# Scores by pairs of heads on two column groups, a fixed order for the first loads, and one piece per kept part of w_in, in an attention + MLP kernel

## The chip, the cores and the metric

The kernel runs on one core of a Trainium2 chip. A core has five engines that run side by side, each with its own queue of instructions in a fixed order: TensorE (PE, matmuls), VectorE (DVE), ScalarE (ACT), GpSimd (POOL) and SyncE (SP, here the main issuer of DMAs). They synchronise through semaphores. DMAs are issued from the queue of an engine and carried out by 16 shared DMA engines. The metric is the device time of one execution in microseconds, lower is better.

## The reference

Inputs are q, k, v of shape 8 x 8 x 576 x 64 (batch, heads, tokens, head size), phi of 8 x 8 x 576 x 32, w_in of 512 x 2048 and w_out of 2048 x 512, all float32.

```python
a    = softmax(phi, axis=memory)                  # 32 memory slots per head
k_m  = einsum('bhsm,bhsd->bhmd', a, k);  v_m = einsum('bhsm,bhsd->bhmd', a, v)
attn = softmax(q @ k_m.T / sqrt(64))              # 576 x 32 per head
x    = (attn @ v_m), heads side by side           # 4608 tokens x 512
out  = relu(x @ w_in) ** 2 @ w_out                # 4608 x 512
```

(The weights arrive as float64 bit patterns, each number as two 32-bit words; the kernel makes from each number a float32 high part and a low part.)

## The kernel before

**Algebra.** The value side is folded into the weights: instead of attn @ v_m and then @ w_in, the kernel makes `vw = v_m @ w_in` per batch (lines 500 to 546) and multiplies the attention probabilities with it. Large products are made of three float32r matmuls (high x high, low x high, high x low), so most tiles exist as a high and a low part (`ah`/`al`, `gh`/`glo`, `V[:, 0]`/`V[:, 1]`).

**Work units.** A *memory unit* `memory(b, hh)` (line 392) treats four heads of batch b: it loads phi, k and v, takes a softmax over phi, and forms k_m and v_m for the four heads with tiled matmuls: in `pk`, heads s = 0 to 3 write to rows 32s to 32s + 31, on four column groups (`tile_position=(0, 32 * s)`, line 426). The sums over tokens are made at L439, L442 or, for odd batches, L445, where two 64-column groups are used. For batches 0 and 1 (lines 455 to 472) k_m and v_m of the four heads are spread into `kvx` with zeros (times `halves`), turned by two transposes into `pv`, and the first block becomes `kbd`, a 128 x 128 matrix with the key memory of two heads on the diagonal. For batches 2 to 7 (473 to 484) k_m goes through `kvn` and a DVE transpose into `kT`; only v_m is turned by PE. `values` copies the turned v_m into `VT` parts. All memory units and the scores of batches 1 to 7 share one PSUM bank, `pa`, in the order in which the program makes them.

**Scores.** For batches 0 and 1 `first_attention` (588) loads q by head in 256-byte rows (L602) and the last 64 tokens apart (L595), turns q with PE (L613), multiplies with `kbd` (L636, L648), takes the softmax (line 678) and turns the result back (L664, L671) to `ath` and `atl`. For batches 2 to 7 `scores` (551) loads q of four heads in two DMAs with one row of 18 tokens x 64 numbers per partition (L557), turns it with DVE in 32 x 32 blocks (`qT`, L569), makes `kb` from `kT` and a mask (L562), and runs, for each half of the tokens (8 and 10 blocks of 32, so 256 and 320 columns), two matmuls of all 128 rows and columns that add up in PSUM (`psc`, L574): one per half of the head size. DVE turns the scores to token rows (L578), softmax follows, and DVE turns back (L703).

**MLP.** `step(g)` does `mm1` (L740: `h` = attention x vw, then relu and square on ACT and DVE) and `mm2` (L770, L771, L773: adds to four accumulators) for one batch and one of 16 blocks of 128 hidden columns. `mm2_left` (L796) treats the left-over 64 tokens of two batches together.

**Weights.** `decode(kind, j, h, room)` (307) loads a 512 KB piece of raw weights (L322) and makes the two parts with five DVE steps, ACT and, for the first pieces, PE (L350 to L352). The parts of w_out stay in SBUF. Those of w_in are stored to two DRAM tensors, `w_in_hi` and `w_in_lo`, by two DMAs on POOL's queue per piece (L364), and `wi_again` (366) loads them again with two DMAs per piece (L369), in rows of 1 KB, for batch 1 and each later pair of batches.

**Order.** Nothing runs in the order of the code. `Plan` (53) collects every operation with its cost per engine, then `order()` (111) simulates the engines: each takes the ready operation with the smallest `late` time (propagated back from its users, or set by `cap`), less `LEAD` for operations marked `lead`. The resulting order is what is issued. A DMA is an operation of the engine that issues it; it costs 620 ns of that engine's queue (1250 if `two`), passes a wire of 240 bytes per ns and lands `LANDS` later. At the start all loads without a predecessor are ready at once, so `late` alone orders them: phi, k, v of the first memory unit, phi of the second, two raw pieces of w_in, k and v of the second unit, q of batch 0, raw w_out, the left-over q.

## Time and profile before

| | us |
|---|---|
| median of three timed runs (lowest, highest) | 816.61 (813.18, 818.7) |
| the profiled execution's own time | 816.34 |
| its span, first to last instruction | 814.6 |
| PE busy | 776.2 |
| DVE busy | 536.4 |
| ACT busy | 403.1 |
| mean granted PE clock | 0.994 |

How to read the profile: PE is matmuls, PEld its weight loads, SPq DMA issue on SP's queue. `L574` is line 574 of the kernel. A row of a group gives out<-in by tile names, shapes, the count, then busy time in us and the mean length of one in ns, then idle time of the engine just before. A row of the timeline gives start and length in us; `x4` means that four instructions were merged, and a bracket gives the idle time before and what ended it. A matmul of plain float32 is two MATMUL instructions. Lengths of matmuls include pipelining and overlap, so the cost of one is read from start to start.

### The profile page before, as it was taken

What the parts mean: (1) busy time and instruction counts of PE and PEld (TensorE: products, weight loads), DVE (VectorE), ACT (ScalarE), POOL (GpSimd) and SP (SyncE); (2) the same over time, 40 slices, a digit from 0 to 9 for tenths busy, and PEclk for the clock granted to TensorE, in tenths of its full rate; (3) what the DMA queues carried; (4) which work ended last, traced back from release to release, by engine and by line L of the source; (5) the groups of instructions that cost most, each with busy time, mean ns of one, the idle gap of its engine ahead of it and who ended that gap; (6) DMA issues with size and microseconds to landing.
All of it is one profiled execution on the core that took longest, in us unless ns stands there. A gap on an engine that the chain in (4) does not pass through costs nothing.

```text
span 814.6 us, 13267 instructions
## 1 busy us (share of the span) xinstructions
PE 776.2 (95%) x4926; PEld 652.5 (80%) x4926; DVE 536.4 (66%) x1190; ACT 403.1 (49%) x922; POOL 63.8 (8%) x103
## 2 busy tenths in 40 slices
PE   4889999999999999999999999999999999999995
PEld 2567888778887888888778888888788888888884
DVE  4678888783468976766776556877677556864540
ACT  2557766675653465634445355644334355643220
POOL 4012202320100100010000100010000100000000
PEclk9999999999999999999999999999999999999998
DMA  7969967666456523423443433513422433100001
GB/s 225 270 191 286 270 176 239 188 170 191 125 146 189 165 81 105 129 37 90 132 125 88 126 106 104 136 34 91 133 58 70 122 108 104 30 24 29 1 1 64
DMA packets 99716, 101.04 MB, mean 124 GB/s; under 512 B 32260, under 2 KB 85508, under 8 KB 99652
## 3 DMA queue, kind: packets, MB, share of 16 engines
q1 hardware_dynamic: 89188, 81.55, 34.2%
q0 software_dynamic: 10464, 18.65, 8.8%
q8 instruction: 39, 0.64, 0.3%
q14 instruction: 25, 0.20, 0.1%
HBM read 79.17 MB, written 17.83 MB: 119 GB/s over the span
## 4 chain that ended last, share of the span: by engine, by line
PE 73%; DVE 8%; issue 6%; DMA 5%; ACT 4%; SPq 1%; POOL 1%; DVEq 0%; POOLq 0%; ACTq 0%
PE h L740 20%; PE acc L770 12%; PE acc L773 12%; PE acc L771 12%; PE accl L796 5%; PE pvw L536 4%; PE psc L574 3%; PE pkv L426 2%; DMA raw<-in_moe_w_out_dram 1%; DMA phi<-in_phi_dram 1%; ACT vw L260 1%; DMA raw<-in_moe_w_in_dram 1%; DMA wo<-work 1%; DVE glo L750 1%; DVE work L327 1%
## 5 line engine op out<-in xcount | busy, mean ns | idle before, releaser
L740 PE MATMUL h<-ath,vw 128*128 128x320 f32 (+1 forms) x1024 | 211.6, 298 | 1.1 <-ACT r L744 0.6
L770 PE MATMUL acc<-wo,gh 128*128 128x512 f32 x512 | 207.0, 404 | 1.8 <-ACT gh L746 1.6
L771 PE MATMUL acc<-wo,gh 128*128 128x512 f32 x512 | 201.7, 394 | 0.0
L740 PEld LDWEIGHTS h<-ath,vw 128*128 128x128 f32 x1024 | 171.0, 189 | 17.2 <-ACT r L744 1.7
L773 PE MATMUL acc<-wo,glo 128*128 128x512 f32 x512 | 162.1, 405 | 1.7 <-DVE glo L750 1.5
L260 ACT CAST vw<-pvw 64x256 fp32r<-64x256 f32 (+1 forms) x224 | 85.7, 397 | 74.5 <-PE pvw L536 35.4
L545 DVE TENSOR_TENSOR vw<-pvw,vw 64x256 fp32r<-64x256 f32 x192 | 78.8, 420 | 64.8 <-ACT vw L260 62.9
L770 PEld LDWEIGHTS acc<-wo,gh 128*128 128x128 f32 x512 | 96.4, 188 | 23.4 <-ACT gh L746 3.7
L740 PE MATMUL h<-atl,vw 128*128 128x320 f32 (+1 forms) x512 | 109.9, 295 | 0.0
L771 PEld LDWEIGHTS acc<-wo,gh 128*128 128x128 f32 x512 | 96.4, 188 | 16.6
L773 PEld LDWEIGHTS acc<-wo,glo 128*128 128x128 f32 x512 | 89.5, 189 | 19.5 <-DVE glo L750 6.2
L746 ACT ACTIVATE gh<-r 128x512 fp32r<-128x512 f32 x128 | 80.8, 632 | 43.4 <-DVE r L745 37.6
L750 DVE TENSOR_TENSOR glo<-r,gh 128x512 fp32r<-128x512 f32 x128 | 87.5, 684 | 21.4 <-ACT r L748 19.7
L744 ACT ACTIVATE r<-h 128x256 f32<-128x256 f32 (+1 forms) x149 | 60.1, 406 | 56.8 <-PE h L740 53.5
L745 DVE TENSOR_SCALAR r<-h 128x320 f32<-128x320 f32 (+1 forms) x107 | 48.9, 459 | 58.4 <-PE h L740 57.9
L740 PEld LDWEIGHTS h<-atl,vw 128*128 128x128 f32 x512 | 82.5, 189 | 0.7 <-issue 0.2
L747 ACT ACTIVATE gl<-r 128x64 fp32r<-128x64 f32 x128 | 32.8, 256 | 68.5 <-DVE r L745 66.5
L748 ACT ACTIVATE r<-r 128x576 f32<-128x576 f32 x94 | 64.5, 686 | 2.2
L796 PE MATMUL accl<-wo,gl 128*128 128x512 f32 x192 | 52.3, 397 | 0.1
L796 PEld LDWEIGHTS accl<-wo,gl 128*128 128x128 f32 x192 | 35.0, 188 | 7.2 <-DVE o L260 0.5
L536 PE MATMUL pvw<-wi,VTh 128*128 128x256 f32 x192 | 37.3, 286 | 0.6 <-issue 0.3
L749 DVE TENSOR_TENSOR r<-r 128x576 f32<-128x576 f32 x34 | 25.7, 756 | 15.8 <-ACT gh L746 14.4
(137 smaller groups left out, 854.3 us busy)
## 6 DMA issues: line engine op xcount, KB each, us to landing
wi<-w_in_hi SPq DMA_DIRECT2D x56, 256.0 KB
wi<-w_in_lo SPq DMA_DIRECT2D x56, 256.0 KB
KV<-in_k_dram SPq DMA_DIRECT2D x32, 256.0 KB
KV<-in_v_dram SPq DMA_DIRECT2D x32, 256.0 KB
raw<-in_moe_w_in_dram SPq DMA_DIRECT2D x16, 512.0 KB
raw<-in_moe_w_out_dram SPq DMA_DIRECT2D x16, 512.0 KB
q<-in_q_dram SPq DMA_DIRECT2D x24, 288.0 KB
out_dram<-o POOLq DMA_DIRECT2D x20, 256.0 KB, 7.7
```

Source lines behind the costliest of these rows:

```text
L260: nc.scalar.copy(o, i) if e == "ACT" else ENG[e].tensor_copy(o, i)
L536: nc.tensor.matmul(pw()[:, x * SL:(x + 1) * SL], l()[:, 2 * hh + x, :], w(r, x), start=(i == 0), stop=(i == 2))
L545: vec({"DVE": tt(SL)}, lambda e, V=V, pr=pr, src=src: nc.vector.tensor_sub(V()[pr, 1, hh, :], src(), V()[pr, 0, hh, :].bitcast(F32)), [pw, ...
L740: nc.tensor.matmul(p()[:, 0:n], V()[:, l, hh, c0:c0 + P], x()[:, hh, cs], start=(i == 0), stop=(i == 5))
L744: op({"ACT": act(n) - 30, **({} if b < 2 else {"DVE": tt(n)})}, lambda e, cs=cs, n=n, p=p: nc.scalar.activation(r()[:, cs], p()[:, 0:n], A ...
L746: op({"ACT": act(SM)}, lambda e: nc.scalar.activation(gh(), r()[:, 0:SM], AF.Square), [r], [gh])
L748: op({"ACT": act(S), **({} if b < 2 else {"DVE": tt(S)})}, lambda e: nc.scalar.activation(r(), r(), AF.Square) if e == "ACT" else nc.vecto ...
L750: vec({"DVE": tt(SM)}, lambda e: nc.vector.tensor_sub(glo(), r()[:, 0:SM], gh().bitcast(F32)), [r, gh], [glo])
L770: nc.tensor.matmul(a(), gh()[:, c], t()[:, 0], start=f0, stop=False)
L771: nc.tensor.matmul(a(), gh()[:, c], t()[:, 1], start=False, stop=False)
L773: nc.tensor.matmul(a(), glo()[:, c], t()[:, 0], start=False, stop=f1)
L796: nc.tensor.matmul(a(), G()[:, l, :], t()[:, w], start=(ff == 0 and n == 0), stop=(ff == NFF - 1 and n == 2))
```

## The change

1. **Scores of batches 2 to 7** use `kbd`, as batches 0 and 1 do: the special way with `kvn`, `kT`, `vx` and `kb` goes, every memory unit makes `kvx` and two transposes, and `kbd` is kept in a buffer per batch parity and head group. q comes in another layout, `[P, 2, NC, 32]`: for each pair y and head i of the pair, two DMAs (one per half of the head size, 32 numbers) of pieces of 128 bytes, eight DMAs per unit instead of two. The two matmuls of a half no longer add up: each makes the scores of one pair of heads from all 128 rows and 64 columns of `kbd`, on its own column group (`tile_position=(0, 64 * y)`), into its own 64 rows of PSUM.
2. **First loads**: eleven names in `FIRST` give the loads a fixed order through `cap`; the two in `BESIDE` (v of the first unit, phi of the second: four and two DMAs) are issued from ACT's queue.
3. **Kept parts of w_in**: one DRAM tensor in the layout of the tile; one store per piece, when both parts are there, and one reload, in rows of 4 KB.
4. `kvx` has a buffer of its own, and some PE costs in the plan are smaller (600 to 460, 1800 to 1400, 450 to 350).

```diff
-LANDS = {"SP": 1400, "POOL": 4000}
+LANDS = {"SP": 1400, "ACT": 1400, "POOL": 4000}
...
-    def dma(fn, size, r=(), w=(), eng="SP", two=False, **more):
-        e = {"SP": nc.sync, "POOL": nc.gpsimd}[eng]
+    def dma(fn, size, r=(), w=(), eng="SP", two=False, first=None, **more):
+        q_ = {"SP": nc.sync, "ACT": nc.scalar, "POOL": nc.gpsimd}
         issue = 700 if eng == "POOL" else 1250 if two else 620
-        return op({eng: issue}, lambda _: fn(e.dma_start), r=r, w=w, size=size, lat=0, **more)
+        if first in FIRST:
+            eng = "ACT" if first in BESIDE else eng
+            more["cap"] = 10000 * FIRST.index(first) - 1e6
+        return op({eng: issue}, lambda _: fn(q_[eng].dma_start), r=r, w=w, size=size, lat=0, **more)
...
+    FIRST = ["phi 0 0", "k 0 0", "v 0 0", "phi 0 1", "k 0 1", "v 0 1", "q 0 0", "q 0 1", "ql 0", "wi 0", "wo 0"]
+    BESIDE = ["v 0 0", "phi 0 1"]
...
-            for x in (0, 1):
-                dma(lambda d, x=x: d(wi_rows(x, j, h), t()[:, x].bitcast(F32)), 2048 * P, r=[(t, (h, x))], w=[(w_in_parts[x], (j, h))], eng="POOL", lead=True)
+            dma(lambda d: d(w_in_parts()[j, h], t().rearrange("p x c f -> p (x c f)").bitcast(F32)), 4096 * P, r=[t], w=[(w_in_parts, (j, h))], eng="POOL", lead=True)
...
-        for x in (0, 1):
-            dma(lambda d, x=x: d(t()[:, x].bitcast(F32), wi_rows(x, s, hh)), 2048 * P, r=[(w_in_parts[x], (s, hh))], w=[(t, (hh, x))], lead=True)
+        dma(lambda d: d(t().rearrange("p x c f -> p (x c f)").bitcast(F32), w_in_parts()[s, hh]), 4096 * P, r=[(w_in_parts, (s, hh))], w=[t], lead=True)
...
+        op({"PE": 350}, turn_kv, [kvx], [pv], lead=True, lat=300)
+        kbd = kTs[b, hh] = st([P, P], F32, f"kb{b % 2}{hh}", f"kbd{u}")
+        op({"ACT": act(P), "DVE": tt(P)}, lambda e: copy(e, kbd(), pv()[:, 0:P]), [pv], [kbd], lead=True)
...
+    def halves_of(d, dst, src):
+        for u in (0, 1):
+            d(dst[32 * u:32 * u + 32], src[:, 32 * u:32 * u + 32].rearrange("(p c) d -> p c d", c=NC))
...
-        Q = st([P, NC * D], F32, "q", f"q{u}")
-        for x in (0, 1):
-            h0 = 4 * hh + 2 * ((x + b) % 2)
-            dma(lambda d, x=x, h0=h0: d(Q()[64 * x:64 * x + 64], q[b, h0:h0 + 2].rearrange("h (p c) d -> (h p) (c d)", c=NC)),
-                2 * S * D * 4, [], [(Q, x)], lead=True)
+        Q = st([P, 2, NC, 32], F32, "q", f"q{u}")
+        for y in (0, 1):
+            for i in (0, 1):
+                hd = 4 * hh + (2 * (y + b) + i) % 4
+                dma(lambda d, y=y, i=i, hd=hd: halves_of(d, Q()[64 * i:64 * i + 64, y], q[b, hd]), S * D * 4, [], [(Q, (y, i))], two=True, lead=True)
...
-                for x in (0, 1):
-                    nc.tensor.matmul(pq()[:, 0:32 * n], kb()[:, x].rearrange("p h m -> p (h m)"),
-                                     qT()[:, x, 0:n].rearrange("p c t -> p (c t)"), start=(x == 0), stop=(x == 1))
+                for y in (0, 1):
+                    ys = slice(64 * y, 64 * y + 64)
+                    nc.tensor.matmul(pq()[ys, 0:32 * n], kbd()[:, ys], qT()[:, y, 0:n].rearrange("p c t -> p (c t)"),
+                                     start=True, stop=True, tile_position=(0, 64 * y))
```

72 lines of the change are left out of this document (22 added, 50 removed).

## The prediction

> **What bounds the kernel now.** I read the page's busy times first, then busy time by stretch for the first 165 us, then the timeline of the start, and last the timeline around two groups of matmuls.
>
> ```profile
> PE 776.2 (95%) x4926; PEld 652.5 (80%) x4926; DVE 536.4 (66%) x1190; ACT 403.1 (49%) x922; POOL 63.8 (8%) x103
> PE   4889999999999999999999999999999999999995
> PE 73%; DVE 8%; issue 6%; DMA 5%; ACT 4%; SPq 1%; POOL 1%; DVEq 0%; POOLq 0%; ACTq 0%
> ```
>
> TensorE (PE) is the bound: 776 of 814.6 us. In the strip of 40 slices only the first three and the last are below 9. So time comes off in two ways: fewer PE microseconds anywhere after the start, or less PE idle time at the start. Relief on another engine is worth only what it gives PE. The sums below are made against the profiled execution's own 816.34 us, which is 1.7 us over its span of 814.6 and 0.27 us under the median of the three timed runs (816.61).
>
> ```profile
> core 0: us, PE busy (x) PEld busy (x) DVE busy (x) ACT busy (x) POOL busy (x), PEclk, DMA share, GB/s
> 0.00:6.00 6.00, 0.00 (x0) 0.00 (x0) 1.26 (x3) 1.59 (x2) 5.13 (x14) 1.00 0.51 140
> 6.00:15.00 9.00, 4.19 (x82) 2.67 (x82) 3.67 (x8) 1.37 (x2) 2.39 (x3) 1.00 0.85 250
> 15.00:30.00 15.00, 12.93 (x132) 8.47 (x132) 7.10 (x21) 6.42 (x13) 3.38 (x5) 1.00 1.02 292
> 30.00:49.00 19.00, 13.82 (x67) 9.16 (x68) 17.28 (x38) 11.28 (x23) 1.15 (x2) 0.91 0.97 253
> 60.00:100.00 40.00, 39.56 (x300) 31.48 (x299) 34.38 (x75) 29.75 (x64) 9.84 (x14) 1.00 0.91 274
> 100.00:165.00 65.00, 59.52 (x353) 51.59 (x351) 52.33 (x110) 44.37 (x96) 13.60 (x18) 1.00 0.70 208
> ```
>
> Each row gives the length of a stretch, busy time per engine, PE's granted clock, the busy share of the DMA engines and what they moved. Up to 49 us PE is busy 4.19 + 12.93 + 13.82 = 30.9 us, so 18 us are idle. The limit changes inside that stretch. Up to 6 us the DMA engines are half idle. From 15 to 30 us they are full while VectorE (DVE) works 7.1 of 15 us. From 30 to 49 us DVE is the limit with 17.28 of 19. Later, from 100 to 165 us, PE loses 5.5 us more while weights are decoded.
>
> ```profile
> 8.39 0.74 ACT L417 ACTIVATE phi<-phi 128x640 f32<-128x640 f32 x1 [5.98 <-DVE phi L415]
> 8.57 4.86 DMA raw<-in_moe_w_in_dram
> 11.08 1.27 DVE L409 TENSOR_REDUCE mx<-phi 128x128 f32<-128x640 f32 x1 [2.73 <-DMA phi<-in_phi_dram]
> 16.75 5.04 SPq L602 DMA_DIRECT2D q<-in_q_dram  x8
> 19.43 0.30 PE L411 MATMUL pmx<-ident,mx 128*128 128x128 f32 x1 [0.58 <-DVE VTl L494]
> 26.80 2.00 PE L636 MATMUL psc<-kbd,qT 128*128 128x64 f32 x16
> 35.46 0.82 DVE L682 TENSOR_REDUCE red<-S 128x20 f32<-128x640 f32 x1 [1.14 <-ACT S L652]
> 48.62 0.51 PE L740 MATMUL h<-ath,vw 128*128 128x256 f32 x2 [0.61 <-ACT r L744]
> ```
>
> The second line is a piece of the chain of waits, the others are the timeline (start, length). Raw weights arrive at 13.4 us, but what they feed cannot run before the attention of batch 0: its q is issued only at 16.75, its second memory unit has its maximum at 11.1 but the matmul that turns it only at 19.4 (one PSUM bank serves all memory units in turn, and the first unit's tail stood behind decode steps on DVE). Scores come at 26.8, the last softmax begins at 35.5, and `h` runs in a stream from 48.6.
>
> **The change, part by part.**
>
> *Start.* The fixed order puts phi, k, v of both memory units and q ahead of the first raw weights. Bytes from the shapes: phi 295 KB, k 590 KB and v 590 KB per unit, eight q loads of 131 KB, 131 KB of left-over q: 4.1 MB; then 1.05 MB each for `wi 0` and `wo 0`. At the 292 GB/s of the full stretch, from 2 us on, q is in by about 16 us, `wi 0` by 20 instead of 13.4, `wo 0` by 23.5. The six DMAs on ScalarE's queue cost it six issues of 5.04/8 = 0.63 us, 3.8 us in all. They lie in its idle 5.98 us ahead of the exponential at 8.39; without that cover the exponential would slip by up to 3.8 us. On SP's queue the same 3.8 us go, at a time when the DMA engines are 0.51 to 0.85 busy, so k and v of the second unit are issued earlier; what they pass are the raw weights. With no decode step on DVE before 20 us, the first unit's tail closes at about 15, the turn at 19.43 moves there, and scores and softmax come 8 to 10 us earlier; PE's queue, in order, no longer holds that turn behind the decode's matmuls. What is late next is DVE. It has idled 49 - (1.26 + 3.67 + 7.10 + 17.28) = 19.7 us by 49 us. After the change the idle part is, as an estimate, 4.7 us before phi lands plus about 6.5 us in the gaps of two memory units one after the other. The same 29.3 us of DVE work is then done about 9 us earlier, and `h` starts near 40. I take -9 us. Ends: -12 if softmax waits for nothing but q, +6.6 if the raw weights, which land 13.4 to 20 us, decide the first `h`.
>
> *Scores of batches 2 to 7.* Twelve units (six batches, two head groups), each with a half of 256 and one of 320 columns.
>
> ```profile
> 249.56 1.03 PE L574 MATMUL psc<-qT,kb 128*128 128x256 f32 x4
> 250.65 0.39 PE L771 MATMUL acc<-wo,gh 128*128 128x512 f32 x1
> 252.25 1.24 PE L574 MATMUL psc<-qT,kb 128*128 128x320 f32 x4
> 253.56 0.39 PE L771 MATMUL acc<-wo,gh 128*128 128x512 f32 x1
> 253.78 0.39 PE L770 MATMUL acc<-wo,gh 128*128 128x512 f32 x1
> 243.53 0.39 PE L773 MATMUL acc<-wo,glo 128*128 128x512 f32 x1
> 243.85 0.28 PE L445 MATMUL pkv<-ones,asum 128*64 128x1 f32 x4
> 244.41 0.40 PE L740 MATMUL h<-atl,vw 128*128 128x256 f32 x2
> 244.64 0.40 PE L740 MATMUL h<-ath,vw 128*128 128x256 f32 x2
> 244.97 1.43 PE L426 MATMUL pkv<-KV,phi 128*32 128x128 f32 x40
> ```
>
> Lengths of matmuls overlap, so I count from start to start. A 512-column matmul takes 253.78 - 253.56 = 0.22 us. One such matmul stands, left out here, between each psc row and the L771 row; so psc holds PE from 249.56 to 250.65 - 0.22, 0.87 us, and from 252.25 to 253.56 - 0.22, 1.09 us, a quarter of it per pass: 0.216 and 0.27 us. After the change each half has two passes on each of two column groups. Do column groups run at once? The L426 row says yes: 40 passes of 128 columns on four groups last 1.43 us; at half of 0.216 each they would last 4.3 us one after another. But a switch to narrower columns and back costs something, and the L445 row, on two groups of 64, shows it: the matmul at 243.53 hands over at 243.75; after the group two 256-column pairs start 0.23 us apart, so PE is back at 244.41 - 0.23 = 244.18. That is 0.43 us for passes of a single column. I take 0.35 us as fixed, the rest for the passes. The new halves are 0.35 + 2 x 0.216 = 0.78 and 0.35 + 2 x 0.27 = 0.89 us; a unit saves 0.29 us, twelve save 3.5. Ends: -11.7 with no fixed part (half of 1.96 us, twelve times), +8.3 with the fixed part and no overlap (24 x 0.35, nearly).
>
> The Trainium skill, "TensorE: Matmul & The Clock Gate", Part 3, gives the span of packed tiles as one matmul plus about 4 ns per further tile, with no price for entering and leaving the mode. By it the scores would give about -11.6 us and the whole sum would be 799; the 0.43 us of the L445 group speaks against it.
>
> *Memory units of batches 2 to 7.*
>
> ```profile
> L483 PE MATMUL pvt<-ident,vx 128*128 128x128 f32 x12 | 3.6, 298 | 1.8 <-DVE vx L479 1.6
> L459 DVE SCALAR_TENSOR_TENSOR kvx<-pkv,rs,par 128x128 f32<-128x128 f32 x8 | 2.5, 345 | 0.1
> L562 DVE TENSOR_TENSOR kb<-kT,bd 128x256 f32<-128x256 f32 x12 | 5.0, 418 | 0.2
> ```
>
> Each unit turns two blocks instead of one: twelve more transposes of 128 columns in one pass, at 0.216/2 = 0.11 us, +1.3 us (at most 12 x 0.298 = 3.6). On DVE the mask multiply (0.418 us) goes and one kvx step (0.345 us) comes; DVE is not the limit there, so 0.
>
> *Loads of q for batches 2 to 7.* A unit has two loads of long rows now; it gets eight, with pieces of 32 numbers (128 bytes), all on SP's queue.
>
> ```profile
> 252.58 1.20 SPq L557 DMA_DIRECT2D q<-in_q_dram  x2
> 259.53 1.13 PE L574 MATMUL psc<-qT,kb 128*128 128x256 f32 x4 [0.28 <-DVE qT L569]
> 272.05 0.41 ACT L260 CAST ath<-at 128x256 fp32r<-128x256 f32 x1 [3.25 <-DVE at L703]
> 272.39 0.49 PE L740 MATMUL h<-ath,vw 128*128 128x256 f32 x2
> 440.66 0.49 DVE L707 TENSOR_TENSOR atl<-at,ath 128x320 fp32r<-128x320 f32 x1
> 447.99 0.47 PE L740 MATMUL h<-ath,vw 128*128 128x320 f32 x2
> ```
>
> Issue goes from 1.20 to 8 x 0.63 = 5.0 us; behind it on SP queue the weight loads of the next slices. The transfer: 256-byte pieces moved 8 x 131 KB in 5.04 us (the L602 row); if a piece of 128 bytes takes no less, 4,608 pieces take 5.7 us. So a unit's q comes 3.8 to 4.5 us later, and the second unit's load waits for the first unit's transposes, as there is one q buffer. In batch 2 nothing covers that: scores waited for q's transposes at 259.5, and `h` starts 0.34 us after ScalarE begins `ath`. I take +2 (between 0, if the new order fills PE otherwise, and 4.5). In batch 4 attention is done at 441.15 and `h` starts at 447.99: 6.8 us cover it, 0.
>
> *Kept parts of w_in.*
>
> ```profile
> L364 POOL DMA_DIRECT2D w_in_hi<-wi x16 | 12.4, 772 | 56.5 <-ACT wi L260 30.8 <-ACT ath L674 18.7 <-ACT gl L747 3.6
> PE pvw L536 <- issue: 0.3, 1, 0.3
> ```
>
> Sixteen of 32 stores go (16 x 0.772 us on POOL's queue, off the path) and half of the reload issues. Of what PE waits for, the products with reloaded weights have 0.3 us in this row. I take 0; -2 to +1.
>
> Sum: -9 - 3.5 + 1.3 + 2 = -9.2, from 816.34 to 807.1 us, so **807 us**, with 802 to 812 from -12 to -5 at the start and the transposes and q loads at their ends.
>
> **The rivals.**
>
> *A, given back.* PE reaches the later decode stretches 9 us earlier, but these have their own pace: from 60 to 100 us DMA is at 0.91 and DVE at 34.38 of 40, and from 100 to 165 PE already waits 5.5 us. For it: those shares. Against it: DVE has idled 19.7 us before, which is work brought forward. If 2 of the 9 us stay: 816.3 - 2 - 2.2 + 2 = 814.
>
> *B, the switch is hidden.* The fixed 0.35 us overlaps with neighbours: scores give -11.7: 799.
>
> *C, q's small pieces.* The mechanism is q arriving after its cover. It decides from a unit later by more than 6.8 us, that is 8.0 us for its loads. If its 4,608 pieces take twice the 5.7 us above, a unit takes 11.4 us, 10.2 more than now: batch 2 pays 10.2, the five others 3.4 each, together 27: 816.3 - 9 - 2.2 + 27 = 832, slower. Against it: loads of 512 pieces issue in 0.63 us. In "DMA: Bandwidth & Descriptors", Specifications, the Trainium skill puts line rate at 512 bytes and up, with read-modify-write below. By that rule C is the likelier; the L602 row, 208 GB/s for 256-byte pieces against 250 to 292 around it, shows a loss but no halving.
>
> *D, column groups in turn.* 816.3 - 9 + 8.3 + 1.3 + 2 = 819. The L426 row is against it.
>
> **How the numbers follow.** Chances: forecast 0.50, A 0.23, B 0.12, C 0.10, D 0.05. Within 1% (8.2 us, about what a measurement can tell from no change) means 808.4 to 824.8. Three quarters of the forecast's own range lie below 808.4: 0.375 + 0.12 from B is 0.50 faster. C is 0.10 slower. A, D and the rest of the forecast: 0.40 the same. The range runs from B to D, 798 to 819.
>
> **What would show it.** Start right: the second unit's turn near 15 us instead of 19.4, scores before 20, `h` in a stream by 40, and DVE under 13 us idle up to then. Wrong if `h` waits for `vw`. Rival A: PE loses more than 5.5 us from 60 to 165 us. Scores right: start to start 0.78 and 0.89 us for a half, B 0.43 and 0.54, D 1.2 and more. C: a unit's q in later than 8 us after its first issue, and PE waiting for qT in batches 4 to 7. The forecast is wrong outright if the first `h` is not before 46 us.

## The result and the profile after

The changed kernel takes 844.6 us (median of four runs, 841.45 to 845.4) against 815.82 us (813.18 to 818.7) on the same chip: the ratio is 1.0345, 95% interval 1.03 to 1.039. It is slower by 28.8 us where 9 us less were forecast. (Ratios here and below compare runs that no disturbance touched, so they can differ a little from the ratio of two medians.)

The page of the changed kernel: PE's busy time, then the strips of 40 slices for PE and its granted clock.

```profile
PE 790.6 (94%) x4938; PEld 652.7 (77%) x4938; DVE 542.1 (64%) x1190; ACT 397.0 (47%) x910; POOL 49.7 (6%) x87
PE   3889989799999699999999999999999999999995
PEclk9999999899999889999999999999999999999998
```

PE is busy 14.4 us more than before, although the products of the scores are shorter. The strips show where time is lost: a 7 in the eighth slice (147 to 168 us) and a 6 in the fourteenth (274 to 295 us), with a clock of 8 in these and in the fifteenth. Busy time by stretch says the same in numbers; first before, then after (columns as in the prediction).

```profile
0.00:49.00 49.00, 30.95 (x281) 20.30 (x282) 29.31 (x66) 20.66 (x40) 12.04 (x23) 0.97 0.91 250
250.00:310.00 60.00, 59.46 (x320) 50.84 (x319) 48.66 (x106) 29.41 (x74) 3.25 (x6) 1.00 0.51 147
540.00:590.00 50.00, 49.27 (x372) 41.01 (x371) 33.58 (x74) 20.53 (x45) 3.10 (x6) 1.00 0.39 105
```

```profile
0.00:49.00 49.00, 30.66 (x343) 21.74 (x343) 25.73 (x58) 16.71 (x32) 9.27 (x20) 1.00 0.88 242
100.00:165.00 65.00, 57.48 (x320) 50.42 (x319) 48.07 (x100) 41.20 (x89) 7.13 (x10) 0.92 0.64 201
250.00:310.00 60.00, 52.81 (x286) 40.82 (x285) 40.21 (x84) 20.63 (x53) 3.44 (x7) 0.89 0.46 122
540.00:590.00 50.00, 48.02 (x286) 39.02 (x285) 33.61 (x76) 21.73 (x50) 2.96 (x5) 1.00 0.36 84
```

From 250 to 310 us, where the MLP passes from batches 0 and 1 to batch 2, PE loses 6.7 us of busy time and runs part of the rest at half clock. From 100 to 165 us it loses 7.5 us instead of 5.5, at a clock of 0.92.

To place the loss I take the start of the first `h` matmul (L740 before, L722 after) of six of the 128 steps, in each trace, and subtract that of the kernel before. Steps 16 and 24 lie in batches 1 and 0; batch 2, and with it the pair of batches 2 and 3, begins at step 32, batch 4 at step 64, batch 5 at 80, batch 6 at 96 and batch 7 at 112. These lags, in us, are used all through:

| kernel | time | ratio, interval | 16 | 24 | 40 | 72 | 96 | 120 |
|---|---|---|---|---|---|---|---|---|
| after | 844.6 | 1.0345, 1.03-1.039 | 9.6 | 7.0 | 20.9 | 20.7 | 26.0 | 27.8 |
| e1 scores alone | 833.1 | 1.021, 1.017-1.025 | 0.9 | 1.3 | 10.1 | 10.0 | 15.0 | 17.0 |
| e2 order of loads alone | 820.1 | 1.005, 1.003-1.007 | 7.7 | 5.9 | 6.7 | 6.3 | 6.1 | 6.1 |
| e3 the same, one queue | 830.7 | 1.018, 1.014-1.022 | 10.4 | 13.2 | 14.6 | 13.9 | 13.8 | 13.6 |
| e4 kept parts alone | 820.7 | 1.006, 1.003-1.009 | 2.5 | 4.4 | 6.1 | 4.6 | 4.2 | 4.0 |
| e5 e1, q in four row loads | 821.1 | 1.011, 1.007-1.014 | 3.5 | 3.4 | 8.0 | 6.3 | 4.1 | 4.8 |
| e9 e1, q loaded as before | 817.3 | 1.004, 1.000-1.008 | 2.5 | 2.4 | 4.5 | 1.8 | 0.9 | -0.3 |
| e18 before, q in pieces | 828.3 | 1.017, 1.013-1.021 | 0.1 | -0.3 | 8.4 | 9.6 | 12.3 | 12.1 |
| e6 e1, left-overs held back | 834.3 | 1.025, 1.019-1.030 | 2.6 | 2.5 | 9.7 | 9.4 | 14.3 | 16.2 |
| e7 e1, planner's order all through | 831.9 | 1.022, 1.015-1.028 | -9.2 | -8.8 | 2.5 | 9.9 | 9.3 | 15.9 |
| e8 before, planner's order all through | 828.3 | 1.016, 1.011-1.021 | -8.2 | -7.5 | -3.5 | 2.6 | 5.1 | 11.7 |
| e10 before, three prices | 825.6 | 1.012, 1.006-1.018 | 8.4 | 5.9 | 7.9 | 9.3 | 9.5 | 9.3 |
| e19 before, one constant | 821.2 | 1.008, 1.005-1.011 | 3.0 | 2.3 | 7.1 | 6.7 | 6.5 | 6.7 |
| e11 before, held to 230 us | 808.7 | 0.994, 0.991-0.997 | -7.7 | -7.1 | -6.7 | -7.2 | -7.7 | -7.8 |
| e12 e2, held | 806.6 | 0.988, 0.983-0.994 | -7.2 | -9.4 | -8.0 | -8.6 | -9.1 | -9.2 |
| e14 e4, held | 810.3 | 0.993, 0.991-0.996 | -6.4 | -5.3 | -2.7 | -3.9 | -4.1 | -4.3 |
| e15 e2 and e4, held | 807.0 | 0.991, 0.988-0.994 | -5.4 | -7.9 | -6.4 | -6.7 | -6.5 | -6.6 |
| e13 after, held | 829.6 | 1.018, 1.014-1.021 | -6.9 | -7.0 | 5.2 | 5.2 | 10.5 | 12.5 |
| e17 e9, held | 808.8 | 0.992, 0.989-0.995 | -6.4 | -6.0 | -2.1 | -4.8 | -5.7 | -6.8 |

So the changed kernel loses 7 us in the first 200 us and 14 at the first change of pair, where batch 2 begins. Between steps 40 and 72, where batches 3 and 4 begin, it loses nothing. It loses 5 us between 72 and 96 and 2 between 96 and 120; the lag steps up from 20.8 at step 80 to 24.8 at step 104, and from 24.8 at step 114 to 27.8 at step 115. These later losses begin with batches 5 and 7, the second batches of their pairs.

**The products themselves came out as forecast.** Timeline of the changed kernel on PE:

```profile
257.72 0.39 PE L753 MATMUL acc<-wo,gh 128*128 128x512 f32 x1
257.96 0.63 PE L755 MATMUL acc<-wo,glo 128*128 128x512 f32 x2
258.51 0.65 PE L556 MATMUL psc<-qT,kbd 128*64 128x256 f32 x4
259.10 0.50 PE L752 MATMUL acc<-wo,gh 128*128 128x512 f32 x1
259.43 0.40 PE L753 MATMUL acc<-wo,gh 128*128 128x512 f32 x1
260.96 0.28 PE L517 MATMUL pvw<-wi,VTl 128*128 128x256 f32 x1
261.17 0.76 PE L556 MATMUL psc<-qT,kbd 128*64 128x320 f32 x4
261.86 0.50 PE L752 MATMUL acc<-wo,gh 128*128 128x512 f32 x1
262.19 0.40 PE L753 MATMUL acc<-wo,gh 128*128 128x512 f32 x1
```

A 512-column pass takes 0.23 us here (257.72 to 257.96). The two passes of L755 hand over at 257.96 + 2 x 0.23 = 258.42; the pass of L752 ahead of 259.43 began in effect at 259.20: the first half adds 0.78 us. The second: from 260.96 + 0.12 to 262.19 - 0.23, 0.88 us. Forecast were 0.78 and 0.89.

**The start did not.** The timeline of the changed kernel, its first 50 us:

```profile
5.87 1.28 ACT L278 ACT_TABLE_LOAD   x1 [5.87 <-DMA KV<-in_v_dram]
10.63 1.23 DVE L408 TENSOR_REDUCE mx<-phi 128x128 f32<-128x640 f32 x1 [2.92 <-DMA phi<-in_phi_dram]
11.78 0.81 DVE L414 TENSOR_TENSOR phi<-phi,pmx 128x640 f32<-128x640 f32 x1
12.62 0.74 ACT L416 ACTIVATE phi<-phi 128x640 f32<-128x640 f32 x1 [5.15 <-DVE phi L414]
18.21 1.12 SPq L323 DMA_DIRECT2D raw<-in_moe_w_in_dram  x2
19.90 0.45 PE L410 MATMUL pmx<-ident,mx 128*128 128x128 f32 x1 [0.49 <-DVE VTl L475]
30.77 0.36 DVE L325 TENSOR_SCALAR work<-raw 128x512 f32<-128x512 f32 x1
37.50 2.00 PE L618 MATMUL psc<-kbd,qT 128*128 128x64 f32 x16
40.97 0.82 DVE L664 TENSOR_REDUCE red<-S 128x20 f32<-128x640 f32 x1 [0.26 <-ACT S L634]
49.52 0.39 PE L722 MATMUL h<-ath,vw 128*128 128x256 f32 x1 [0.56 <-ACT ath L649]
```

ScalarE's queue holds its table load behind the DMA issues, but this is not what holds the first exponential: ScalarE is idle for 5.15 us just before it, until VectorE has done the first unit's subtraction (11.78). On VectorE that subtraction stands behind the second unit's maximum, which waits for its phi until 10.63. The kernel before starts the subtraction 0.51 us after the matmul ahead of it (7.53 and 7.02); that matmul starts at 7.77 here, so the subtraction could have started at about 8.3, an estimate. Of the 4.2 us by which the exponential is late, 3.5 are thus the order on VectorE and 0.7 the later start of the first maximum (5.55 us instead of 4.80). The first exponential is at 12.62 us instead of 8.39, the second unit's turn at 19.90 instead of 15 as forecast, the last softmax begins at 40.97 instead of 35.46, and the stream of `h` begins at 49.52, not at 40. The raw weights, issued at 18.21, are decoded from 30.77. Up to 49 us VectorE has done less than before, 25.73 us of work instead of 29.31.

**At the first change of pair** the timeline of the changed kernel reads:

```profile
260.09 5.33 SPq L531 DMA_DIRECT2D q<-in_q_dram  x8
273.85 4.34 PE L778 MATMUL accl<-wo,gl 128*128 128x512 f32 x18
276.92 0.71 DVE L550 STREAM_TRANSPOSE qT<-q 128x512 f32<-128x512 f32 x1
278.47 0.65 PE L556 MATMUL psc<-qT,kbd 128*64 128x256 f32 x4
280.65 0.76 PE L556 MATMUL psc<-qT,kbd 128*64 128x320 f32 x4
284.42 0.85 DVE L526 TENSOR_TENSOR vw<-pvw,vw 64x256 fp32r<-64x256 f32 x2
285.37 0.48 PE L517 MATMUL pvw<-wi,VTh 128*128 128x256 f32 x2 [3.30 <-issue]
288.65 0.58 PE L722 MATMUL h<-ath,vw 128*128 128x256 f32 x1 [2.32 <-ACT ath L260]
```

The second unit's q is issued from 260.09, and the last of its 4,608 packets of 128 bytes ends at 267.9, 7.8 us later. But its transpose runs on VectorE only at 276.92, and its scores at 278.47 and 280.65, behind 43 and 46 of the 48 left-over products `accl` (6 and 11 before). Those products used to fill PE while the softmax ran; now they are spent, PE waits 3.30 and 2.32 us, and its clock is halved from 286.6 until 300 us. The second wait is for the softmax (`ath`). The profile names nothing that ended the first; VectorE's work on the `vw` that PE had made before, spread among the steps of the softmax, ends at 285.27, just ahead of it.

**Later batches.** In batch 7 the end of the first unit's scores, the start of the second unit's and the first `h`, then the first two of these in the kernel before:

```profile
724.18 0.75 PE L556 MATMUL psc<-qT,kbd 128*64 128x320 f32 x2
738.75 0.65 PE L556 MATMUL psc<-qT,kbd 128*64 128x256 f32 x4
746.25 0.38 PE L722 MATMUL h<-ath,vw 128*128 128x256 f32 x1 [0.18 <-DVE r L727]
```

```profile
698.39 1.24 PE L574 MATMUL psc<-qT,kb 128*128 128x320 f32 x4
702.25 1.02 PE L574 MATMUL psc<-qT,kb 128*128 128x256 f32 x4
```

The second unit's scores come 14.6 us after the first unit's last, instead of 3.9, and end 4.6 us before batch 7 begins, instead of 13.8. From there on PE waits a few times for VectorE's `r`, up to 0.59 us. In batch 4 the second unit's scores are as late (18.5 us instead of 5.4) and cost nothing.

### The profile page after: what moved, and what is told of

Same layout as the page of the kernel before. It is cut to its first block, busy times and chain, and to the rows that moved or that the text cites. A ratio compares the mean times of both kernels' runs of the same rounds, so it can differ in the third digit from the quotient of the medians.

```text
span 842.4 us, 13311 instructions
## 1 busy us (share of the span) xinstructions
PE 790.6 (94%) x4938; PEld 652.7 (77%) x4938; DVE 542.1 (64%) x1190; ACT 397.0 (47%) x910; POOL 49.7 (6%) x87
## 5 line engine op out<-in xcount | busy, mean ns | idle before, releaser
L722 PE MATMUL h<-ath,vw 128*128 128x320 f32 (+1 forms) x1024 | 217.0, 304 | 10.3 <-ACT r L726 4.9
L752 PE MATMUL acc<-wo,gh 128*128 128x512 f32 x512 | 206.4, 403 | 0.8 <-ACT gh L728 0.5
L722 PEld LDWEIGHTS h<-ath,vw 128*128 128x128 f32 x1024 | 171.9, 191 | 30.8 <-ACT r L726 6.6
L755 PE MATMUL acc<-wo,glo 128*128 128x512 f32 x512 | 160.2, 404 | 0.4 <-DVE glo L732 0.4
L752 PEld LDWEIGHTS acc<-wo,gh 128*128 128x128 f32 x512 | 97.3, 190 | 24.9 <-ACT gh L728 3.1
L722 PE MATMUL h<-atl,vw 128*128 128x320 f32 (+1 forms) x512 | 113.0, 300 | 0.3 <-DVE atl L657 0.2
L753 PEld LDWEIGHTS acc<-wo,gh 128*128 128x128 f32 x512 | 97.3, 190 | 18.5 <-issue 1.0
L732 DVE TENSOR_TENSOR glo<-r,gh 128x512 fp32r<-128x512 f32 x128 | 87.8, 686 | 32.6 <-ACT r L730 29.3
L755 PEld LDWEIGHTS acc<-wo,glo 128*128 128x128 f32 x512 | 89.8, 189 | 21.3 <-issue 4.3
L722 PEld LDWEIGHTS h<-atl,vw 128*128 128x128 f32 x512 | 84.3, 192 | 1.9 <-DVE atl L657 0.5
L730 ACT ACTIVATE r<-r 128x576 f32<-128x576 f32 x88 | 60.3, 685 | 2.0
L731 DVE TENSOR_TENSOR r<-r 128x576 f32<-128x576 f32 x40 | 30.2, 755 | 18.4 <-ACT gh L728 12.5
```

The lines of the kernel that those rows point to most:

```text
L722: nc.tensor.matmul(p()[:, 0:n], V()[:, l, hh, c0:c0 + P], x()[:, hh, cs], start=(i == 0), stop=(i == 5))
L730: op({"ACT": act(S), **({} if b < 2 else {"DVE": tt(S)})}, lambda e: nc.scalar.activation(r(), r(), AF.Square) if e == "ACT" else nc.vecto ...
L732: vec({"DVE": tt(SM)}, lambda e: nc.vector.tensor_sub(glo(), r()[:, 0:SM], gh().bitcast(F32)), [r, gh], [glo])
L752: nc.tensor.matmul(a(), gh()[:, c], t()[:, 0], start=f0, stop=False)
L753: nc.tensor.matmul(a(), gh()[:, c], t()[:, 1], start=False, stop=False)
L755: nc.tensor.matmul(a(), glo()[:, c], t()[:, 0], start=False, stop=f1)
```

## The experiments

**One part at a time.** e1 is the kernel before with the change to the scores, e2 with the order of the first loads, e3 with the order but `BESIDE` empty, e4 with the kept parts. e2 and e3, and with them e12 and e15 below, also have the smaller planner prices for batches 0 and 1, which e10 tries alone.

The first lines of each, in this order, against the kernel before; e3 against e2:

```diff
-        Q = st([P, NC * D], F32, "q", f"q{u}")
+        Q = st([P, 2, NC, 32], F32, "q", f"q{u}")
...
+    FIRST = ["phi 0 0", "k 0 0", "v 0 0", "phi 0 1", "k 0 1", "v 0 1", "q 0 0", "q 0 1", "ql 0", "wi 0", "wo 0"]
+    BESIDE = ["v 0 0", "phi 0 1"]
...
-    BESIDE = ["v 0 0", "phi 0 1"]
+    BESIDE = []
...
+    w_in_t = dram.tile([NSL, 2, P, 4 * SL], F32, name="w_in_parts")
```

> The kernel before with the change to the scores of batches 2 to 7 alone (pairs of heads on two column groups, the eight q loads of 128-byte pieces per unit); the loads at the start and the kept parts of w_in as before. Theory Q (q's loads): in the trace of the changed kernel the lag grows by 12 to 13 us where the pair of batches 2 and 3 begins, by 4 to 5 and by 3 where the next two pairs begin, and the scores give about 2 us back in between. If q's loads and where they place the scores are the cause, this kernel is late by these alone: 816 + 12.5 + 4.5 + 3 - 2 = 834 us, and PE runs at half clock for over 10 us around 290. Rival (the start or the kept parts cause the transitions): this kernel only has the shorter scores and twelve more transposes, 816 - 3.4 + 1.3 = 814 us, with no half clock around 290.

> The kernel before with the order of the first loads alone, six of them on ScalarE's queue. Theory S (the start is worth the 7 to 9 us by which the changed kernel is late until 250 us, and nothing later): 816 + 8 = 824 us, first scores of the second unit near 37 us instead of 31. Rival (the order is harmless or gains once nothing else is changed, and the lag of the start comes from the single stores of w_in): 807 to 816 us. Rival 2 (a late start also sets up the later transitions, as the decode stretches and the stores shift): 836 us or more.

> As the kernel with the order of the first loads alone, but all of them on SP's queue, none on ScalarE's. Theory S1 (the loss is ScalarE's: its six issues stand ahead of its table load and of the first exponential, which moved from 8.39 to 12.62 us, and the second phi lands early and puts its maximum ahead of the first unit's subtraction on VectorE): without them the first exponential is back near 8.4 us and the kernel gains at least 5 us on the kernel with both queues, 816 to 819 us. Rival S2 (the loss is the order itself: the raw weights come 17 us later, so the decode that used to fill VectorE and PE early stands behind the attention of batch 0): no gain over the kernel with both queues, 822 to 827 us.

> The kernel before with the kept parts of w_in in one piece alone: 16 stores instead of 32 and one reload of 512 KB instead of two of 256 KB. Theory Q and S both hold that this part is worth nothing: 815 to 817 us. Rival (a store now waits for both parts of a decoded piece, and a reload for all of it, so that the products with reloaded weights at the pair transitions come later): 3 to 5 us slower, 819 to 821 us, with more PE idle time ahead of the products with reloaded weights.

Measured: e1 833.1, e2 820.1, e3 830.7, e4 820.7 us, which is 17.4, 4.4, 15.0 and 5.1 over the before of that chip, 815.65. e1, e2 and e4 sum to 27 of the 28.8. e1 shows the losses after step 24 alone; the theory on q's loads stands so far (what its text takes for the beginnings of the next two pairs are the beginnings of batches 5 and 7). e2 lies between its theory and its rivals and decides for none. e4 went to the rival's number; whether for the rival's reason is settled below, by e14. e3 refutes both theories for the start, as it is 10 us slower than e2. Its timeline:

```profile
15.61 0.45 PE L418 MATMUL pmx<-ident,mx 128*128 128x128 f32 x1 [1.35 <-DVE VTl L501]
28.22 2.00 PE L643 MATMUL psc<-kbd,qT 128*128 128x64 f32 x16
31.26 0.26 ACT L659 COPY S<-pscl 128x128 f32<-128x128 f32 x1
35.83 1.26 DVE L416 TENSOR_REDUCE mx<-phi 128x128 f32<-128x640 f32 x1
38.53 0.81 DVE L689 TENSOR_REDUCE red<-S 128x20 f32<-128x640 f32 x1
```

Without ScalarE's queue the first unit's subtraction is back ahead of the second unit's maximum, the first exponential is at 8.29 us, and the second unit's turn does come at 15.61, as the prediction had it. But its scores, complete at 31.5 us, wait 7 us on VectorE, behind decode steps and even behind the first maximum of batch 1 (35.83): the decode that used to run ahead of this softmax now shares VectorE with it.

**Is q's transfer the cause, or its place?** e5 is e1 with q in four loads of 32 whole rows and the planner's prices left as they are in e1, e6 is e1 with the left-over products held behind the scores that the planner puts ahead of them, e7 and e8 hold PE, VectorE and ScalarE to the planner's list, in e1 and in the kernel before. The section on the kernel before says that the planner's order is what is issued; that is not quite so. The planner calls the operations in its order, but the library that builds the five queues orders once more: in e1 the planner has 18 left-over products ahead of the second unit's first scores, the built program 48.

The edits of e5, of e6, and of e7 and e8:

```diff
-                dma(lambda d, y=y, i=i, hd=hd: halves_of(d, Q()[64 * i:64 * i + 64, y], q[b, hd]), S * D * 4, [], [(Q, (y, i))], two=True, lead=True)
+                dma(lambda d, y=y, i=i, hd=hd: d(Q().rearrange("p y c d -> p (y c d)")[32 * (2 * y + i):32 * (2 * y + i) + 32],
+                                                 q[b, hd].rearrange("(p c) d -> p (c d)", c=NC)), S * D * 4, [], [(Q, (y, i))], two=True, lead=True)
```

```diff
+            if scored is not None:
+                after_that(i, scored)
```

```diff
+            if o.left in ("PE", "DVE", "ACT"):
+                if o.left in behind:
+                    tc.add_manual_dep(i, behind[o.left].name, ...)
+                behind[o.left] = i
```

> The kernel with the change to the scores alone, but q of batches 2 to 7 comes in four loads of 32 whole rows (4,608 bytes each) per unit instead of eight loads of 128-byte pieces. q then does not lie as the products need it: this kernel leaves the arrangement of q out, so its scores of batches 2 to 7 are of the wrong parts; everything else is done. Theory O (the order in the built program is the cause: in batch 2 the second unit's scores stand behind all 48 left-over products there, behind 6 of them in the kernel before, and here behind 30): the scores come 18 x 0.22 = 4 us earlier than with the pieces, and the loss of 13 us at the first transition shrinks to 5 to 9: 824 to 830 us. Rival P (the transfer of the small pieces is the cause): with long rows all of it goes, 814 to 817 us. Rival G (the column groups, the transposes or the masks are the cause, whatever loads q): no change, 832 to 834 us.

> The kernel with the change to the scores alone, all loads and products as there, but on PE the left-over products are held behind the scores that the planner puts ahead of them: 18 of 48 stand ahead of the second unit's scores of batch 2 instead of 48. Theory O: q was in at 260.4 us and its scores started only at 269.4; they now start near 262 to 264, PE has the remaining 30 left-over products for the time of the softmax, and 7 to 10 of the 13 us at the first transition come back: 823 to 826 us, with less than 7 us at half clock around 280. Rival P (q's transfer): nothing comes back, PE waits for q instead, 831 to 835 us.

> The kernel with the change to the scores alone, with PE, VectorE and ScalarE held to the planner's own order all through. Theory O: the first transition improves as with the left-over products held behind, and the second and third too, 815 to 823 us; the planner's own list ends at 801.7 us for this kernel and at 811.4 for the one before. Rival (the planner's prices are off by too much to be followed to the letter: an engine held to the list waits wherever an operation comes later than its price): 835 us or more, with waits spread over the whole run.

> The kernel before, with PE, VectorE and ScalarE held to the planner's own order all through: the control for the same with the changed scores. Theory O: here the built order differs little from the planner's where it matters (the second unit's scores of batch 2 stand behind 6 left-over products in both), so 812 to 820 us. Rival (following the list costs by itself): 825 us or more, and the difference to the same with the changed scores tells what these are worth in the same order; by the measured lengths of the products that is 2 to 4 us.

Measured: 821.1, 834.3, 831.9, 828.3. Against the before of its own chip e5 is 7.5 us late where e1 is 17.4, so long rows give 10 us back; its runs spread from 818.5 to 831.1 us, and its median lies between the order theory and the transfer theory. e6 missed: 18 left-over products ahead of the second unit's scores instead of 48 gave nothing back, because VectorE, whose order was left alone, ran the second unit's transpose of q only at 267.25, and PE waited for it. So the place of the left-over products alone is not the cause. e7 and e8 missed as well. They were 8 to 9 us ahead of the kernel before at steps 16 and 24, which no theory had said, and lost more than that later. In the planner's order the kernel with the new scores still lost 11 us between steps 24 and 40, against 4 in e8, although its second unit's last scores stand where e8's do (255.4 us against 255.9). It ran at half clock for 13.65 us there and e8 not at all, which can cost up to half of that, 6.8 us, an estimate. At the end the two differ by 3.5 us.

**Old and new products, old and new loads.** e9 is e1 with q loaded as in the kernel before; e18 is the kernel before with q loaded as in the changed one.

The edit of e9; that of e18 puts the lines with the minus, in their loops, into the kernel before:

```diff
-                hd = 4 * hh + (2 * (y + b) + i) % 4
-                dma(lambda d, y=y, i=i, hd=hd: halves_of(d, Q()[64 * i:64 * i + 64, y], q[b, hd]), S * D * 4, [], [(Q, (y, i))], two=True, lead=True)
+            h0 = 4 * hh + 2 * ((x + b) % 2)
+            dma(lambda d, x=x, h0=h0: d(Q().rearrange("p y c d -> p (y c d)")[64 * x:64 * x + 64], q[b, h0:h0 + 2].rearrange("h (p c) d -> (h p) (c d)", c=NC)),
+                2 * S * D * 4, [], [(Q, x)], lead=True)
```

> The kernel with the change to the scores alone, but q of batches 2 to 7 comes as before the change: two loads of 64 whole rows per unit, with the planner's price for these. q then does not lie as the products need it, so the scores of batches 2 to 7 are of the wrong parts; everything else is done. With four loads of rows at the price of the eight pieces the kernel took 821 us. Theory L (all that the scores lose comes from q's loads, from when they land and from the place that a late landing gives the scores among PE's work): now only the products are changed, 815 - 3.4 + 1.3 = 813 us, between 811 and 816, and PE has no waits of over 1 us and no half clock between 250 and 310 us. Rival G (the column groups, the second transpose or the narrower chain on VectorE cost something at the transitions too): 818 to 822 us, with idle time on PE near 275 us.

> The kernel before with q of batches 2 to 7 loaded as in the changed kernel, eight loads of 128-byte pieces per unit, and nothing else changed: products, masks and transposes are the old ones. q then does not lie as they need it, so the scores of batches 2 to 7 are of the wrong parts. It closes the square: old products with old loads 815 us, new products with old loads 817, new products with new loads 833. Theory L (the loads are the whole loss): 828 to 834 us, with waits on PE and half clock between 260 and 300 us. Rival (the new loads only hurt together with the shorter products, which leave PE less to do while q and the softmax are under way): 816 to 822 us.

Measured: 817.3 and 828.3. The loads alone, with the old products, lose 13.6 us; the products alone, with the old loads, 3 us at the edge of the interval. So the loads are the larger part of e1's 17.4, as far as single kernels tell; what a mere reshuffle can do is seen in e10 and e19 below, and the runs with a held start decide. e9 still had a wait of 2.28 us and half clock from 277 to 284 us, against the theory's letter. In e18 the second unit's halves stand like this:

```profile
263.33 1.17 PE L579 MATMUL psc<-qT,kb 128*128 128x256 f32 x4 [0.39 <-DVE qT L574]
265.74 5.01 PE L801 MATMUL accl<-wo,gl 128*128 128x512 f32 x21
270.59 1.29 PE L579 MATMUL psc<-qT,kb 128*128 128x320 f32 x4
```

Here 24 left-over products went between the two halves, 21 of them in one stretch. The start of that last half, against 262.15 us before, is late by 8.4 us in e18, 9.4 in e1, 7.8 in e5, 9.8 in e6 and 18.5 in the changed kernel, and the lag at step 40 is 8.4, 10.1, 8.0, 9.7 and 20.9: the lag goes with the place that the last half of the scores of batch 2 has on PE. That this place decides is not shown: e9 has 2.7 and 4.5, e19 (below, old loads and old products) 3.7 and 7.1, and e7, in the planner's order, -6.7 and +2.5.

**Is the start a property of the parts?** e10 changes three planner prices that are also in the change (the third, of L664, goes from 600 to 460 like the first), and no instruction; e19 one constant. e11 and e12 hold PE, VectorE and ScalarE to the planner's list for what it starts before 230 us, in the kernel before and in e2.

```diff
-                op({"PE": 600}, turn, [(Q, 2 * x), (Q, 2 * x + 1)], [pq], lead=True, lat=300)
+                op({"PE": 460}, turn, [(Q, 2 * x), (Q, 2 * x + 1)], [pq], lead=True, lat=300)
...
-            op({"PE": 1800}, mm, [qT, kbd], [pc], lead=True, lat=300)
+            op({"PE": 1400}, mm, [qT, kbd], [pc], lead=True, lat=300)
```

```diff
-LEAD = 9000
+LEAD = 9200
```

```diff
+        if o.start > 230000 or o.left not in ("PE", "DVE", "ACT"):
+            continue
```

> The kernel before with nothing changed but three prices in the planner (the q transposes and the transposes back of batches 0 and 1 at 460 instead of 600 ns, their score products at 1400 instead of 1800): no instruction is added, removed or changed, only the order in which the planner places the work of the first two batches can move. Theory R (the first 250 us are sensitive to any shift of the order, because decode, attention and the loads share PE, VectorE and one queue, so that the 4 to 6 us that the kept parts cost alone, and as many of the order of the loads, are a reshuffle and no price of these edits): the time moves by 2 to 6 us in either direction. Rival K (the order is robust, and the 5 us of the kept parts are their own): 815 us, within 1.5.

> The kernel before with one constant of the planner changed, LEAD from 9000 to 9200 ns: no instruction is added, removed or changed, only the order of the work can move, here also at the transitions. Theory R (the time depends on how the order happens to fall, by several us): 816 to 828 us, more likely slower than faster, since the kernel before was kept for its time; with three changed prices it was 825.6. Rival (the 11 us of the three prices were peculiar to these): 815 us, within 2.

> The kernel before, with PE, VectorE and ScalarE held to the planner's own order, but only for what the planner starts before 230 us of its own time; the rest is placed as before. Held all through, the kernel before was 7 to 12 us ahead of itself at 160 to 240 us and lost that and 12 us more later. Theory R (the built order of the first 230 us is worse than the planner's, and what comes later does not depend on it): 815 - 8 = 807 us. Rival (the gain is given back at the first transition, since attention of batch 2 waits for its loads): 813 to 816 us.

> The kernel with the order of the first loads alone, six on ScalarE's queue, with PE, VectorE and ScalarE held to the planner's own order for what it starts before 230 us. Theory R (the order of the loads loses by the reshuffle that it sets off): held to the planner's list, which ends 3.9 us earlier than for the kernel before, it is as fast as the kernel before held in the same way or up to 4 us faster, 803 to 808 us. Rival S (the order of the loads costs by itself, through the raw weights that come 17 us later and the exponential that comes 4 us later): 4 us or more slower than the kernel before held in the same way, 811 us or more.

Measured: e10 825.6, e19 821.2, e11 808.7, e12 806.6. Three prices cost 11 us by the medians (0.6 to 1.8% by the interval), more than the order of the loads or the kept parts cost by themselves, and more than the 2 to 6 us of the theory. No instruction comes or goes, but besides the order the planner also chooses anew which of two engines runs an operation: VectorE has 1,190 instructions in the kernel before, 1,188 in e10 and 1,184 in e19, and ScalarE as many more. e19 loses 4.8 us between steps 24 and 40, with the old loads. Held, the order of the loads (with the three prices) is 2.1 us faster than the kernel before held in the same way, by medians; the intervals overlap. The stretches of e12:

```profile
100.00:165.00 65.00, 64.22 (x383) 57.17 (x382) 49.30 (x100) 46.87 (x101) 11.64 (x15) 1.00 0.57 173
250.00:310.00 60.00, 59.73 (x330) 51.53 (x329) 47.93 (x106) 30.96 (x79) 2.70 (x5) 1.00 0.43 133
```

The gain is in the decode stretch: PE loses 0.8 us there instead of 5.5, at full clock, and nothing is given back at the change of pair.

**The parts with the start held.** e13 is the changed kernel, e14 e4, e15 e2 and e4 together, e17 e9, all held to the planner's list before 230 us by the edit of e11.

> The changed kernel, all three parts, with PE, VectorE and ScalarE held to the planner's own order for what it starts before 230 us. Theory: two losses that add up, the reshuffle of the first 250 us and q's loads of batches 2 to 7. Holding the order takes the first away (the order of the loads held in this way took 806.6 us), the second stays, as 43 of 48 left-over products still stand ahead of the second unit's scores of batch 2: 806.6 + 17 = 824 us, 820 to 828. Rival (the transitions only lose because they are reached late and out of step, so that a good start mends them): 806 to 812 us.

> The kernel with the kept parts of w_in in one piece alone, held to the planner's order before 230 us. Theory R (the 5 us that the kept parts cost by themselves were a reshuffle): as the kernel before held in the same way, 808.7 us, within 2.5. Rival K (a store waits for both parts, a reload for all of it, and that costs whatever the order): 812 us or more.

> The order of the first loads with ScalarE's queue and the kept parts in one piece, without the change to the scores, held to the planner's order before 230 us. Theory R: the two parts cost nothing of their own once the order is held, 804 to 809 us, about 1% faster than the kernel before. Rival: the two disturb each other at the start, where POOL's stores and the raw weights share the DMA engines: 812 us or more.

> The changed products of the scores with q in two loads of whole rows as before (q does not lie as the products need it, so the scores of batches 2 to 7 are of the wrong parts), held to the planner's order before 230 us; start and kept parts as in the kernel before. Theory L (the products are worth what their lengths say, -3.4 + 1.3 us, if q's loads are as before): 808.7 - 2 = 806.5 us, 804 to 809. Rival G (the products bring nothing even then, as PE waits at the transitions for the softmax chain instead): 809 to 814 us, with idle time on PE near 275 us.

Measured: 829.6, 810.3, 807.0, 808.8. The kept parts, 5.1 us slower alone, differ from e11 by 1.6 us when held, inside the intervals: most of the 5.1 was a reshuffle. The changed kernel comes out just above its theory's 828. It gains 15 us from the held start, where the kernel before gains 6, so the distance between the two shrinks from 28.8 to 20.9 us. It keeps the loss at the first change of pair, 12 us between steps 24 and 40, and the later ones. e13 and e15 differ in the change to the scores alone, and both are held: 22.6 us, with lags that differ by 0.9 us at step 24, 11.6 at 40, 11.9 at 72, 17.0 at 96 and 19.1 at 120. The new products with the old loads come to e11's time, at the border between theory and rival: their 2.1 us did not show; by the ratios they are worth 0.2%, within the intervals. So with the start held the loss comes with the new loads of q, and with nothing else that was changed; the old products with the new loads were not tried held. e12 and e15 beat both kernels, e15 at 0.991 (0.988 to 0.994), e12 at 0.988 (0.983 to 0.994).

## Why the prediction was wrong

**Start, -9 forecast, about +7 by the lag at step 24.** Two steps failed. The six issues on ScalarE were costed at nothing, with 3.8 us if the cover went. The cover held, as ScalarE was still idle for 5.15 us before the exponential; what slipped it by 4.2 us was the order on VectorE, which the sum does not have. The step that carried the nine microseconds was "The same 29.3 us of DVE work is then done about 9 us earlier": it took VectorE's work as a sum, free of order, and in the changed kernel only 25.73 us of it were done by 49 us. e3 has the turn at the forecast's place and still begins the last softmax 3 us later than before, since the decode, which had run in VectorE's gaps ahead of it, now lies across it. Held, where this is settled by the planner's list, the order of the loads with the three prices is worth about -2, not -9. And what the sum left out altogether is that an edit can make planner and library place the work anew: e10 and e19 moved the time by 11 and 6.5 us without adding or removing an instruction. With the start held, the distance between the two kernels is 20.9 us (e13 against e11), so some 8 of the 28.8 are the order of the start, and 21 are left.

**Scores of batches 2 to 7, -3.5 and +1.3.** The mechanism and the lengths were right, rivals B and D fell. The Trainium skill, "TensorEngine Tiling (Array Packing)", Key Properties, says that a change of tiling mode drains TensorE; the rows above agree in so far as two overlapped passes of 0.22 us take 0.78 us between full-size products. But the saving is not seen in the time of e9 or e17.

**Loads of q, +2.** This was the term that decided. It was costed for batch 2 as a delay of 3.8 to 4.5 us of which half would be filled, and at 0 elsewhere; measured, over e18, e1 and the changed kernel, are 9 to 14 us at the first change of pair, 3 to 5 where batch 5 begins and up to 2 where batch 7 begins, of which e19 shows that up to 5 at the first can come without any change of the loads. With the start held it is 22.6 us in all (e13 against e15). The step that failed is "So a unit's q comes 3.8 to 4.5 us later": it took the landing of q for the delay of the scores. In batch 2 the second unit's scores begin 18.9 us later than before (278.47 against 259.53), 12 more than the kernel's own lag at step 24. For batch 4 the forecast's 0 was right, but batches 5 and 7 were not looked at. (The 5.7 us for 4,608 pieces also rest on a misreading: the 5.04 us of the row of L602 are the time in which its eight DMAs were issued, not that in which their bytes moved.) Rival C had the sign, and its 10.2 us for batch 2 are near the measured 9 to 14; but its mechanism, q arriving after its cover, is not what the trace of batch 2 shows, and that its sum of 27 us comes near is luck. A unit's q took 7.8 us from first issue to last packet, between the forecast's 5.7 and rival C's 11.4, and just under the 8.0 from which C was to decide. The packets of the changed kernel take, as medians, 13 ns for 128 bytes, 18 for 256, 27 for 512 and 159 for 4,096, so 128 bytes move at half the rate of 512; but q had been in for 9 us when its transpose ran. The Trainium skill's rule quoted there ("DMA: Bandwidth & Descriptors", Specifications), line rate from 512 bytes up, agrees with the loss below 512; above, the trace still gains, from 19 bytes per ns at 512 to 26 at 4,096, and the measurement decides. What was missed is that another form of load moves the work that waits for it to other places in the queues: here the second unit's transposes and scores come later, behind 37 more left-over products, and PE has nothing to fill the softmax with after that. By what rule planner and library place them so is not shown.

**Kept parts, 0.** Right when held, within the 1.6 us that can't be told from nothing; +5 when not, most of it a reshuffle.

**Rival A** saw PE's loss from 60 to 165 us rise; it did, to 7.5 us after 100 us, but in a start that was already late. The chance of 0.10 for slower came from C alone; a case "the order falls worse" was missing, and e10 shows that it should have been among them, with up to 11 us to the slow side. (One slip that changes little: of the range 802 to 812 not three quarters lie below 808.4 but about two thirds.)

## What to carry to other kernels

Where a list scheduler places the work, an edit's price is not only its own length: measure the edit with the order held, and a change of a few planner prices with no edit at all, before believing a difference of 1%. A load that becomes slower should be costed by where the work that waits for it ends up in the queues, and by whether filler is left for the wait behind that. Here the largest gain seen was not from any part of the change but from holding the order of the first 230 us: 6 us in the kernel before, 15 in the changed one.

## What the runs showed of the hardware

**The clock follows PE's idle share in windows of 3.41 us.** Stretches of e1 around its waits at the first change of pair:

```profile
272.00:273.60 1.60, 0.30 (x3) 0.00 (x0) 1.26 (x3) 0.44 (x2) 0.00 (x0) 1.00 0.93 166
273.70:287.30 13.60, 8.32 (x29) 6.72 (x29) 8.02 (x18) 3.33 (x9) 0.00 (x0) 0.50 0.46 110
287.40:297.40 10.00, 10.00 (x53) 7.63 (x54) 7.09 (x15) 4.53 (x12) 0.00 (x0) 1.00 0.08 13
```

Changes of the granted clock lie whole multiples of 3.413 us apart; here the clock is halved from 273.66 to 287.31, four windows. I counted PE's idle time in each such window after 60 us, in the traces of both kernels and of the 18 experiments: each of the 22 changes to half clock follows a window with 1.60 to 3.41 us idle, and no window of full clock with 1.87 us or more went without one. The Trainium skill, "TensorE: Matmul & The Clock Gate", Part 1, gives the same free-running window of 3413 ns, but speaks of a whole idle window; in this case about half a window was enough, and between 1.60 and 1.87 us it went either way. So a wait of 2 us can cost more than itself: e1's 8.32 busy us at half clock are some 4 us of work at full clock, an estimate. How much of the loss at the first change of pair is clock and how much the wait was not tried apart.

**A granted clock of 0.95 that slowed nothing.** The profiled run of e18 has it in the records almost throughout; its stretch from 310 to 540 us, then that of the kernel before:

```profile
310.00:540.00 230.00, 228.55 (x1391) 194.24 (x1389) 152.63 (x345) 114.08 (x273) 7.65 (x14) 0.95 0.39 102
```

```profile
310.00:540.00 230.00, 228.58 (x1395) 194.94 (x1394) 156.98 (x355) 114.42 (x275) 7.65 (x14) 1.00 0.36 102
```

In these 230 us the lag of e18 grew by about 1 us, where 5% of the clock would be 11 us. The record and the pace disagree, and the runs do not say why.
